# Eight early gate/up half blocks for nine, and the query side's exponential-times-key-sum product on GpSimd

## The chip, the cores and the metric

The kernel runs on one core of a Trainium2 chip. The metric is the time of one execution on the device, in microseconds (us), as the median of several runs. Engines are named as in the profile: PE is TensorE (matmuls; PEld its weight loads), DVE is VectorE, ACT is ScalarE, POOL is GpSimd, SP is SyncE, which issues most DMAs. Each engine works through its own queue in order; semaphores make it wait for the others.

## What is computed

With x of 2048 rows by 576 columns, 32 heads of 18 and a hidden width of 4608, all in f32:

```python
xn = layernorm(x)
q, k, v = split(xn @ wqkv)                       # 32 heads of 18
pq, pk = q @ w_phi, k @ w_phi                    # per head
phi_q = [softmax(pq), softmax(-pq)]; phi_k = [softmax(pk), softmax(-pk)]
kv = phi_k^T v;  z = sum over rows of phi_k      # per head
o = (phi_q kv) / (phi_q z + 1e-6)
s = o @ wo
g = silu((silu(xn @ w_gate) * (xn @ w_up)) @ w_down)
out = x + s * g
```

## The kernel before

**Stages.** A first stage normalizes x and prepares weights (0 to 60 us of the span). A key/value stage makes phi_k, kv and z (to 216 us). A *query stage* makes phi_q, o and s (its transposes run to 447 us). Then comes the gated network: hidden width in NF = 36 blocks of 128 columns, first for rows 0 to 1023 (half i = 0, to about 1010 us), then for rows 1024 to 2047 (i = 1), and a short finish. Matmul operands are split into a high part and a low part, so that a product is made of several matmuls: `split` (lines 72 to 74) casts on ACT and subtracts on DVE.

**Blocks of gate and up.** `gate_up` makes one block of one half by a recursive scheme of 7 products instead of 8, each of 7 matmuls of 512 columns (`product`, line 1014). Some half blocks are made early instead, in the plain way, by `early_tile` (lines 141 to 153; matmuls in line 108): for two row groups j, a gate and an up product of 14 matmuls each, a SiLU (line 147), a product on DVE (line 151) and a store to `h_dram`. They give TensorE work while the attention stages wait on other engines. `EARLY` is the number of blocks that are early in half 1, `FIRST = (EARLY + 1, EARLY)` the number in half 0 and half 1: five and four, nine half blocks. In the network's stage, an early half block is loaded by `stored` instead of being made.

**Weights of the other blocks.** `gate_up_weights` makes a block's parts from raw weights the first time and keeps them in `w_dram` for half 1; a block that was early in half 0 but isn't in half 1 is made there from raw weights. The last rows of the weights are handled apart: `tails(n)` prepares a group of four blocks, with four subtractions on POOL (lines 810 to 813), a cast on ACT (815), a difference on DVE (816) and twelve DMAs issued by POOL (819) into `t_dram`. There are `TAILS` = 8 groups, each tied to a query tile.

**The query stage** works on 16 tiles of 128 rows, in pairs. `q_tile` makes 28 matmuls of 288 columns into `p` (line 108); then on DVE the maximum and minimum per head (530) and two differences (531); two exponentials on ACT (534) into `e`; on DVE the sums of `e` per head (538), the product `ez` of `e` and the key sums `zb` (832), its sums per head (834), five small steps (836 to 841) and the scaling of `e` (842). `numer` transposes `e` of both tiles of a pair on TensorE (854) for each of five groups of heads, splits the result (`ph` on ACT, `pl` on DVE), multiplies it by kv (861) and splits again (`oh`, `ol`); `project` multiplies by wo (889). For each pair the program gives the numerator of the pair before, the two query tiles, then the projection.

**What sets the order.** The kernel is written with a tile framework that orders each engine's instructions itself, when the program is built: by priority (position in the program, raised by `high_priority`) among what it takes to be ready, with `issue_after` as an extra condition. So a change in one engine's load changes the order on all of them. Early matmuls fill the places where TensorE would wait.

Of the kernel before, what the change touches and what calls it, by code (L numbers as in the profile page):

```python
# [23 lines left out]
NF = F // P  # L24
# [5 lines left out]
NL = GROUPS[-1][1]  # L30
NK = NL + NL // 2
QS = 256
EARLY = 4
FIRST = (EARLY + 1, EARLY)
TAILS = (NF - EARLY + 3) // 4
LAG = 3
SHORT = range(22, NF - 5, 4)
# [15 lines left out]
def heads(ap):  # L53
    return ap.rearrange("p (h d) -> p h d", d=DH)


def spread(ap, n):
    return ap.unsqueeze(2).to_broadcast([P, n, DH])
# [3 lines left out]
def gated_hedgehog_kernel(ctx: ExitStack, tc, x, w_qk, w_v, consts_in, wo, w_gu, w_tail, w_down, out):  # L62
# [5 lines left out]
    nc = tc.nc  # L68
# [7 lines left out]
    def split_rows(hi, lo, src):  # L76
        nc.scalar.copy(hi, src)
        nc.vector.tensor_sub(lo, src[:, :, 0:2], hi[:, :, 0:2])
        nc.vector.tensor_sub(hi[64:96, :, 2], src[64:96, :, 2], hi[64:96, :, 2])
# [6 lines left out]
    s_dram = dram.tile([S, D], F32, name="s_dram")  # L86
    h_dram = dram.tile([2, FIRST[0], P, HS], F32, name="h_dram")
    x_dram = dram.tile([2, 4, P, 4, P], F32, name="x_dram")
    sum_dram = dram.tile([2, P, 4, 4, 5, P], F32, name="sum_dram")
    w_dram = dram.tile([NF - EARLY, P, 7, 4, P], F32, name="w_dram")  # L90
    t_dram = dram.tile([TAILS, 4, 3, 32, 7, P], F32, name="t_dram")
# [3 lines left out]
    def block(t):  # L95
        return t // HT, (t % HT) // 4, slice((t % 4) * P, (t % 4 + 1) * P)

    def xw(ps, i, j, cols, wh, wl, stationary_x):
        pairs = []
        for k in range(2):  # L100
            b = XB[i][2 * j + k]
            for c in range(2):
                pairs += [(b[:, c, cols], w[:, k, c]) for w in (wh, wl)]
                pairs += [(b[:, 3 + c, cols], wh[:, k, c])]
            pairs += [(b[:, 2, cols], wh[:, k, 2])]
        for n, (a, b) in enumerate(pairs):
            l, r = (a, b) if stationary_x else (b, a)
            last = nc.tensor.matmul(ps, l, r, start=n == 0, stop=n == len(pairs) - 1)  # L108
        return last
# [9 lines left out]
    def early_raw_part(f, m):  # L119
        raw = epool.tile([P, 2, 3, P], F32, name="raw", bufs=2)  # L120
        nc.sync.dma_start(raw, w_gu[f, :, m:m + 2])
        return raw

    def early_place():
        return epool.tile([P, 2, 3, P], F32R, name="wh", bufs=3), epool.tile([P, 2, 2, P], F32R, name="wl", bufs=3)

    def early_weights(f, *behind):
        parts = []
        for m in (0, 2):
            raw = early_raw_part(f, m)  # L130
            parts.append(early_place())
            with ExitStack() as order:
                for b in behind:
                    order.enter_context(tc.issue_after(b.ins))
                with tc.high_priority():
                    split_rows(*parts[-1], raw)
        return parts
# [3 lines left out]
    def early_tile(f, i, parts, js=(0, 1), banks=None, store=nc.sync, behind=None):  # L141
        for j in js:
            pg, pu = banks or [eps.tile([P, BT], F32, name="pe") for _ in range(2)]
            xw(pg, i, j, slice(0, BT), *parts[0], False)
            h = epool.tile([P, BT], F32, name="h")
            with tc.high_priority():
                silus.append(nc.scalar.activation(h, pg, AF.Silu))
            last = xw(pu, i, j, slice(0, BT), *parts[1], False)
            with tc.issue_after(behind.ins) if behind else ExitStack():
                with tc.high_priority():  # L150
                    nc.vector.tensor_mul(h, pu, h)
            store.dma_start(h_dram[i, f, :, j * BT:(j + 1) * BT], h)
        return last

    outs = []
    with ExitStack() as att:
# [18 lines left out]
        with ExitStack() as wst:  # L175
# [4 lines left out]
            with ExitStack() as pst:  # L180
# [15 lines left out]
                xns, ws, wv, halves = {}, {}, {}, {}  # L196
# [328 lines left out]
            def softmax_parts(ps, e):  # L525
                m = kk_pool.tile([P, 2, H], F32, name="m", bufs=1)
                p4 = ps[:, :, 0:HALF].rearrange("p a (h d) -> p a h d", d=DH)
                for s, op in enumerate((ALU.max, ALU.min)):
                    m3 = m[:, s].rearrange("p (a h) -> p a h", a=2)
                    nc.vector.tensor_reduce(m3, p4, axis=AX.X, op=op)  # L530
                    read.append(nc.vector.tensor_sub(e[:, s * D:(s + 1) * D].rearrange("p (a h d) -> p a h d", a=2, d=DH),
                                                     p4, m3.unsqueeze(3).to_broadcast([P, 2, H // 2, DH])))
                for s in range(2):
                    last = nc.scalar.activation(e[:, s * D:(s + 1) * D], e[:, s * D:(s + 1) * D], AF.Exp,
                                                scale=1.0 if s == 0 else -1.0)
                exps.append(last)
                sm = kk_pool.tile([P, 2 * H], F32, name="sm")
                nc.vector.reduce_sum(sm, heads(e), axis=AX.X)
                return sm
# [142 lines left out]
            order = [6, 7, 0, 1, 2, 3, 4, 5]  # L682
# [63 lines left out]
        with ExitStack():  # L746
# [3 lines left out]
            zb = qc.tile([P, 2 * D], F32, name="zb")  # L750
# [33 lines left out]
        with ExitStack() as qst:  # L784
# [38 lines left out]
            def q_tile(t):  # L823
                i0, j0, cols = block(t)
                pq = qps.tile([P, 2, 512], F32, name="p2")
                for i in range(2):
                    w = slice(i * HALF, (i + 1) * HALF)
                    xw(pq[:, i, 0:HALF], i0, j0, cols, QH[:, :, :, w], QL[:, :, :, w], True)
                e = qk.tile([P, 2 * D], F32, name="e", bufs=4)
                r = softmax_parts(pq, e).rearrange("p (s h) -> p s h", s=2)  # L830
                ez = qk.tile([P, 2 * D], F32, name="ez", bufs=1)
                nc.vector.tensor_mul(ez, e, zb)
                y = qk.tile([P, 2 * H], F32, name="y")
                nc.vector.reduce_sum(y, heads(ez), axis=AX.X)
                y2 = y.rearrange("p (s h) -> p s h", s=2)
                nc.vector.scalar_tensor_tensor(y2[:, 0], r[:, 0], DEN_EPS, y2[:, 0], op0=ALU.mult, op1=ALU.add)
                nc.vector.tensor_mul(y2, y2, r[:, ::-1])
                den = qk.tile([P, H], F32, name="den")
                nc.vector.tensor_add(den, y2[:, 0], y2[:, 1])
                nc.vector.reciprocal(den, den)  # L840
                nc.vector.tensor_mul(y2, r[:, ::-1], den.unsqueeze(1).to_broadcast([P, 2, H]))
                last_e.append(nc.vector.tensor_mul(heads(e), heads(e), spread(y, 2 * H)))
                return e
# [54 lines left out]
            order = list(range(S // QS // 2, S // QS)) + list(range(S // QS // 2))  # L898
# [13 lines left out]
                with tc.issue_after(last_e[3 * n // 2 + 2].ins):  # L912
                    tails(n, exps[NT + 3 * n // 2 + 2])

        for f, halves in [(1, (0,)), (0, (0,))] + [(f, (1, 0)) for f in range(2, EARLY)]:
            parts = first_weights.pop() if f == 1 else early_weights(
                f, *{0: read[2 * NT + 1:2 * NT + 2], 2: (read[2 * NT + 3], exps[NT + 1])}.get(f, ()))
            for i in halves:
                early_tile(f, i, parts, (1,) if f == 1 else (0, 1), behind=read[2 * NT + 1] if f == 1 else None)
# [38 lines left out]
    def gate_up_weights(i, f, ld=None):  # L958

        parts, wt = {}, wts[0]  # L960
        wts.reverse()
        n, q = divmod(f - EARLY, 4)
        raw = i == 0 or f < FIRST[0]
        if raw:
# [3 lines left out]
        def ready(m, src):  # L968
            k = 1 if m == 6 else 2
            w = fw.tile([P, k, 4, P], F32R, name=f"w{k}", bufs=2 if k == 1 else 4)  # L970
            if not raw:
                nc.sync.dma_start(w.bitcast(F32), w_dram[f - EARLY, :, m:m + k])
            else:
# [16 lines left out]
        else:  # L990
            ready(2, ld[:, 2:4] if raw else None)
        held = {0: silus[-2:-1], 2: tops[0:1], 3: tops[1:2]}.get(f - FIRST[0]) if i == 0 else None

# [6 lines left out]
        elif i == 0 and f in SHORT:  # L1000
            later.append(lambda: last(copies[-1:]))
        elif (i, f) == (0, FIRST[0] + 3):
            opened.append(lambda: ready(6, ld[:, 1:2]))
# [416 lines left out]
    for i in range(2):  # L1420
        order = [NF - 1] * i + list(range(FIRST[0], NF - i))
        if i:
            order.insert(NF // 2, EARLY)
        for f in range(FIRST[i]):
            order.insert(4 * f + 1 - i, f)
        units += [(i, n, f) for n, f in enumerate(order)]
# [34 lines left out]

    todo = [(i, f) for i, n, f in units if f >= FIRST[i] and (i == 0 or f < NF - 1)]
    kept = []
    parts = early_weights(EARLY)
    first_rows = [acc[:, 1].rearrange("p (a b) n -> p a (b n)", a=2)[:, n] for n in range(2)]
    for t, f in zip(first_rows, (FIRST[0], 0)):
        nc.sync.dma_start(t, w_down[f * P:(f + 1) * P, :])
    xo = operands(0)
    early_tile(EARLY, 0, parts, store=nc.gpsimd)
    early_raw = [raw_weights(f) for _, f in todo[0:2]]  # L1470
    with tc.issue_after(outs[-3].ins):
        ready = [gate_up_weights(*todo.pop(0), early_raw.pop(0))]
# [84 lines left out]
```

## Time and profile before

| | |
|---|---|
| median of 3 runs | 1579.47 us (1579.38 to 1579.89) |
| the profiled execution | 1580.98 us, its span 1579.2 us |
| granted TensorE clock | 1.00 |
| PE, DVE, ACT, POOL busy | 99%, 74%, 46%, 43% of the span |
| matmuls recorded | 9371 |

A profile's page groups instructions by line, engine, operation and tiles; "x16 | 21.6, 1350 | 0.0" reads: sixteen of them, 21.6 us in all, 1350 ns on average, no idle time of the engine ahead of them. A matmul is recorded with its whole way through the array, while the next one follows sooner: the pace is read from a chain, "1.59 PE px L1014 x7".

### The profile page before, as it was taken

How to read it: one execution, taken by the hardware profiler on the slowest of the kernel's cores; microseconds unless marked ns; L12 is line 12 of the kernel's file. 1: busy time of each engine (PE TensorE's matmuls, PEld its weight loads, DVE VectorE, ACT ScalarE, POOL GpSimd, SP SyncE). 2: the span in 40 equal slices, each digit the busy share in tenths (PEclk: the TensorE clock that was granted, in tenths of full speed). 3: DMA queues.
4: the chain of work that ended last, by engine and by line, in shares of the span. 5: the costliest groups of instructions: out<-in, count | busy, mean ns of one | idle time of the engine just before them, and what ended most of it. 6: DMA issues, size and time to landing. Idle time of an engine off the chain costs nothing.

```text
span 1579.2 us, 25305 instructions
## 1 busy us (share of the span) xinstructions
PE 1570.4 (99%) x9371; PEld 1415.5 (90%) x9371; DVE 1162.8 (74%) x1722; ACT 729.0 (46%) x1408; POOL 671.5 (43%) x723
## 2 busy tenths in 40 slices
PE   9999999999999999999999999999999999999998
PEld 7999999999988898898888888888888888888887
DVE  7777769999947787987777778545766667666577
ACT  6633344545445644444544444454333343333334
POOL 5766653334125545563644444313323324133133
PEclk9999999999999999999999999999999999999999
DMA  9424343336357455454545543964545655555445
GB/s 284 142 67 165 135 154 117 105 118 209 120 185 259 159 181 198 161 182 174 186 161 202 177 168 125 355 210 139 155 146 157 193 173 161 175 184 187 145 118 182
DMA packets 123287, 269.05 MB, mean 170 GB/s; under 512 B 12436, under 2 KB 54100, under 8 KB 121884
## 3 DMA queue, kind: packets, MB, share of 16 engines
q1 hardware_dynamic: 110572, 246.57, 47.6%
q0 software_dynamic: 3552, 12.59, 2.8%
q10 hardware_dynamic: 9040, 8.28, 1.6%
q8 instruction: 74, 1.21, 0.3%
q14 instruction: 49, 0.40, 0.1%
HBM read 167.54 MB, written 99.09 MB: 169 GB/s over the span
## 4 chain that ended last, share of the span: by engine, by line
PE 96%; POOL 1%; DVE 1%; DMA 1%; issue 1%; ACT 0%; SPq 0%; DVEq 0%; POOLq 0%; ACTq 0%
PE px L1014 25%; PE pd L1136 25%; PE pw L1014 12%; PE p L108 6%; PE py L1014 6%; PE pe L108 5%; PE p L889 4%; PE kvp L547 2%; PE pt L861 2%; PE pe L50 1%; PE vx L636 1%; PE pt L854 1%; PE tp L50 1%; PE vw L636 1%; DMA wst<-in_A_w_qk 0%
## 5 line engine op out<-in xcount | busy, mean ns | idle before, releaser
L1136 PEld LDWEIGHTS pd<-dw,hh 128*128 128x128 f32 x3000 | 421.8, 188 | 19.8 <-DVE acc L1372 0.8
L1136 PE MATMUL pd<-dw,hh 128*128 128x288 f32 x3000 | 435.7, 294 | 0.0
L1014 PE MATMUL px<-X,w 128*128 128x512 f32 x1512 | 385.6, 390 | 0.0
L1014 PEld LDWEIGHTS px<-X,w 128*128 128x128 f32 x1512 | 274.6, 188 | 46.1
L1014 PE MATMUL pw<-X,w 128*128 128x512 f32 x744 | 188.8, 389 | 0.0
L1014 PEld LDWEIGHTS pw<-X,w 128*128 128x128 f32 x744 | 139.5, 188 | 28.9
L1372 DVE TENSOR_TENSOR acc<-pd,acc 128x576 f32<-128x576 f32 x128 | 96.4, 753 | 93.3 <-PE pd L1136 92.6
L1047 DVE TENSOR_TENSOR s<-pw,s 128x512 f32<-128x512 f32 x126 | 86.4, 687 | 89.5 <-ACT s L1042 78.9
L1042 ACT COPY s<-px 128x512 f32<-128x512 f32 x126 | 73.6, 584 | 144.9 <-PE px L1014 144.7
L73 ACT CAST hh<-ha 128x512 fp32r<-128x512 f32 x139 | 82.2, 620 | 94.2 <-PE pd L1136 68.7
L74 DVE TENSOR_TENSOR hh<-ha,hh 128x512 fp32r<-128x512 f32 x139 | 111.8, 829 | 18.8 <-ACT hh L73 18.5
L1344 POOL TENSOR_TENSOR hb<-hb 128x512 f32<-128x512 f32 x34 | 46.6, 1372 | 157.2 <-DVE hb L1059 156.8
L74 DVE TENSOR_TENSOR w<-ld,w 128x512 fp32r<-128x512 f32 (+1 forms) x96 | 76.9, 803 | 38.6 <-ACT w L73 37.7
L1014 PE MATMUL px<-X,wt 128*128 128x512 f32 x252 | 98.0, 389 | 0.0
L1014 PE MATMUL py<-X,w 128*128 128x512 f32 x378 | 96.5, 390 | 0.0
L1357 POOL TENSOR_TENSOR ha<-ha 128x512 f32<-128x512 f32 x34 | 52.3, 1554 | 100.1 <-DVE hh L74 94.7
L1331 POOL TENSOR_TENSOR h<-ha,hb 128x512 f32<-128x512 f32 x34 | 44.5, 1309 | 107.2 <-DVE ha L1063 76.4
L983 POOL TENSOR_TENSOR ts<-ld 128x256 f32<-128x256 f32 x32 | 26.8, 839 | 139.6 <-issue 67.4
L73 ACT CAST w<-ld 128x512 fp32r<-128x512 f32 (+1 forms) x96 | 52.7, 550 | 70.3 <-POOL ld L986 40.6
L1067 ACT COPY py<-px 128x512 f32<-128x512 f32 x63 | 36.0, 572 | 106.1 <-PE px L1014 94.6
L108 PE MATMUL pe<-X,wh 128*128 128x512 f32 x260 | 80.4, 395 | 0.0
L1014 PEld LDWEIGHTS py<-X,w 128*128 128x128 f32 x378 | 68.3, 188 | 10.8
(325 smaller groups left out, 3242.3 us busy)
## 6 DMA issues: line engine op xcount, KB each, us to landing
w_dram<-w SPq DMA_DIRECT2D x90, 512.0 KB, 2.6
w<-w_dram SPq DMA_DIRECT2D x90, 512.0 KB, 4.3
wt<-t_dram SPq DMA_DIRECT2D x62, 336.0 KB, 4.4
ld<-in_B_w_gu SPq DMA_DIRECT2D x32, 512.0 KB, 6.3
rt<-in_B_w_down SPq DMA_DIRECT2D x33, 288.0 KB, 5.1
rb<-in_B_w_down SPq DMA_DIRECT2D x33, 288.0 KB, 3.3
w_dram<-w SPq DMA_DIRECT2D x30, 256.0 KB, 2.1
w<-w_dram SPq DMA_DIRECT2D x30, 256.0 KB, 2.7
```

Source lines behind the costliest of these rows:

```text
L73: cast = nc.scalar.copy(hi, src)
L74: return cast, nc.vector.tensor_sub(lo, src, hi)
L108: last = nc.tensor.matmul(ps, l, r, start=n == 0, stop=n == len(pairs) - 1)
L889: nc.tensor.matmul(ps[:, 0:HALF], a, bw, start=k == 0, stop=k == len(mm) - 1)
L1014: nc.tensor.matmul(ps, l, r, start=first and n == 0, stop=last and n == len(mm) - 1, skip_group_check=True)
L1042: snaps.append(nc.scalar.copy(t, ps))
L1047: nc.vector.tensor_add(t, ps, t)
L1136: nc.tensor.matmul(ps, l, r, start=first and n == 0 and m == 0, stop=n == len(hs) - 1 and m == 2, skip_group_check=True)
L1331: sub(s, g["h"][0][0], g["h"][0][1])
L1344: nc.gpsimd.tensor_add(a21, a21, g["h"][1][1])
L1357: sub(a12, a12, g["h"][0][0])
L1372: adds.append(nc.vector.tensor_add(a2, pd[:, :, 0:HALF], a2))
```

## The change

`EARLY` becomes 3 and `FIRST` (5, 3): the early half blocks are now blocks 0 to 4 in half 0 and 0 to 2 in half 1, eight in all. Block 3 of half 1 is made by `gate_up` from raw weights, as block 4 was already; `w_dram` and `t_dram` begin with block 3, so that `TAILS` becomes 9. The product `ez` is issued to POOL.

```diff
-EARLY = 4
-FIRST = (EARLY + 1, EARLY)
+EARLY = 3
+FIRST = (EARLY + 2, EARLY)
 TAILS = (NF - EARLY + 3) // 4
...
                 ez = qk.tile([P, 2 * D], F32, name="ez", bufs=1)
-                nc.vector.tensor_mul(ez, e, zb)
+                nc.gpsimd.tensor_mul(ez, e, zb)
                 y = qk.tile([P, 2 * H], F32, name="y")
                 nc.vector.reduce_sum(y, heads(ez), axis=AX.X)
...
-        for f, halves in [(1, (0,)), (0, (0,))] + [(f, (1, 0)) for f in range(2, EARLY)]:
+        for f, halves in [(1, (0,)), (0, (0,))] + [(f, (1, 0)) for f in range(2, EARLY)] + [(EARLY, (0,))]:
...
         if i:
-            order.insert(NF // 2, EARLY)
+            for f in range(EARLY, FIRST[0]):
+                order.insert(NF // 2 + 4 * (f - EARLY), f)
...
-    parts = early_weights(EARLY)
+    parts = early_weights(FIRST[0] - 1)
...
-    early_tile(EARLY, 0, parts, store=nc.gpsimd)
+    early_tile(FIRST[0] - 1, 0, parts, store=nc.gpsimd)
```

Three places show how the order changes. On DVE, at tile 4 (the second of pair 2), where the row L842 scales `e` of tile 3 and `tl` belongs to a tail, before:

```order
L842 TENSOR_TENSOR e<-e,y 128x1152
L531 TENSOR_TENSOR e<-p_2704,m 128x576
L816 TENSOR_TENSOR tl<-tl,th 128x896
L538 TENSOR_REDUCE sm<-e 128x64
L832 TENSOR_TENSOR ez<-e,zb 128x1152
L834 TENSOR_REDUCE y<-ez 128x64
L836 SCALAR_TENSOR_TENSOR y<-sm,y 128x32
```

and after:

```order
L531 TENSOR_TENSOR e<-p_2704,m 128x576
L841 TENSOR_TENSOR y<-sm,den 128x64
L842 TENSOR_TENSOR e<-e,y 128x1152
L74 TENSOR_TENSOR ol<-pt,oh 126x256
L538 TENSOR_REDUCE sm<-e 128x64
L834 TENSOR_REDUCE y<-ez 128x64
L816 TENSOR_TENSOR tl<-tl,th 128x896
L836 SCALAR_TENSOR_TENSOR y<-sm,y 128x32
```

L832 is gone from DVE, and L834, which now waits for POOL, stands directly behind L538; L816 has moved behind both.

On TensorE, at the end of tile 6's products (`p_2967`), before:

```order
L108 MATMUL p_2967<-QL,X_67 128x288
L108 MATMUL p_2967<-QH,X_67 128x288 x2
L108 MATMUL pe<-X_67,wl 128x512
L861 MATMUL pt<-ph,KVH 126x256 x2
L861 MATMUL pt<-ph,KVL 126x256 x2
L861 MATMUL pt<-pl,KVH 126x256 x2
L889 MATMUL p<-WOH,oh 128x288
```

and after:

```order
L108 MATMUL p_2967<-QH,X_67 128x288 x2
L108 MATMUL p_2967<-QL,X_67 128x288
L108 MATMUL p_2967<-QH,X_67 128x288 x2
L889 MATMUL p<-WOH,ol 128x288
L889 MATMUL p<-WOH,km 128x288
```

Eleven of the 56 projections L889 now stand ahead of these products, with the last L861 of the numerator; 45 follow them.

On POOL, in the query stage, as a piece of the difference (before with -, after with +):

```order
+L832 TENSOR_TENSOR ez<-e,zb 128x1152 x2
+L819 DMA t_dram<-th 32x896 x7
+L832 TENSOR_TENSOR ez<-e,zb 128x1152
+L819 DMA t_dram<-th 32x896
 L819 DMA t_dram<-tl 32x896 x4
 L819 DMA t_dram<-th 32x896 x8
+L832 TENSOR_TENSOR ez<-e,zb 128x1152
 L819 DMA t_dram<-tl 32x896 x4
+L832 TENSOR_TENSOR ez<-e,zb 128x1152
```

The sixteen `ez` now stand among the issues of the tails' DMAs.

## The prediction

> **What bounds the kernel now.** I read the page's busy table first, then a table of windows, then the chain of waits around one pair of query tiles.
>
> ```profile
> span 1579.2 us, 25305 instructions
> PE 1570.4 (99%) x9371; PEld 1415.5 (90%) x9371; DVE 1162.8 (74%) x1722; ACT 729.0 (46%) x1408; POOL 671.5 (43%) x723
> core 0: us, PE busy (x) PEld busy (x) DVE busy (x) ACT busy (x) POOL busy (x), PEclk, DMA share, GB/s
> 219.00:437.00 218.00, 217.62 (x1464) 202.38 (x1464) 202.33 (x314) 107.37 (x175) 71.13 (x134) 1.00 0.46 142
> 437.00:478.00 41.00, 41.00 (x225) 35.08 (x224) 19.36 (x29) 18.09 (x35) 13.19 (x17) 1.00 0.62 207
> 478.00:1555.00 1077.00, 1077.00 (x5968) 956.49 (x5967) 763.49 (x1096) 486.00 (x957) 428.90 (x388) 1.00 0.54 177
> ```
>
> TensorE has work all the time at a granted clock of 1.00: a matmul saved is time saved, and a TensorE wait added is time lost. The one stretch with a second engine near its limit is 219 to 437 us, the query stage, where DVE is busy 202.33 of 218 us (93%). The change touches just this stage. The profiled execution took 1580.98 us, 1.8 more than its span; the median of the three runs shown, 1579.47, lies 1.5 below it. I add the sum to 1580.98 and take 1.5 off.
>
> Pair 3 (tiles 5 and 6) shows how closely the two engines run together. First TensorE's chain, then DVE's rows (start, length).
>
> ```profile
> 287.59 1.60 PE p L108 x12
> 290.13 7.44 PE p L889 x56
> 297.57 0.22 PE pt L854 x2
> 297.79 3.72 PE p L108 x28
> 301.51 1.16 PE pe L108 x5
> 302.67 0.39 PE pt L854 x2
> ```
>
> ```profile
> 290.17 0.75 DVE L530 TENSOR_REDUCE m<-p 128x32 f32<-128x576 f32 x1
> 290.83 0.42 DVE L74 TENSOR_TENSOR ol<-pt,oh 126x256 fp32r<-126x256 f32 x1
> ...
> 292.85 0.76 DVE L531 TENSOR_TENSOR e<-p,m 128x576 f32<-128x576 f32 x1
> ...
> 294.16 1.36 DVE L842 TENSOR_TENSOR e<-e,y 128x1152 f32<-128x1152 f32 x1
> 295.44 1.34 DVE L538 TENSOR_REDUCE sm<-e 128x64 f32<-128x1152 f32 x1
> 296.70 1.35 DVE L832 TENSOR_TENSOR ez<-e,zb 128x1152 f32<-128x1152 f32 x1
> 298.08 1.35 DVE L834 TENSOR_REDUCE y<-ez 128x64 f32<-128x1152 f32 x1
> ...
> 301.08 1.52 DVE L842 TENSOR_TENSOR e<-e,y 128x1152 f32<-128x1152 f32 x1
> ```
>
> Tile 6's products end at 289.19; the transposes that need its finished `e` begin at 302.67; the last DVE step on `e` ends at 302.60. TensorE arrives 0.07 us after the data. Its own work in between (56 products L889, two transposes, 28 products of tile 7, five early ones) fills 13.5 us. Over the stage it loses almost nothing to this:
>
> ```profile
> PEld pt L861 <- DVE pl L74: 1.1, 5, 0.3
> PEld pt L854 <- DVE e L842: 0.6, 2, 0.4
> ```
>
> So there is no reserve: DVE's chain and TensorE's program end together.
>
> **The change part by part.**
>
> *One early half block less, one more in the recursive form.* An early half block is 2 x 2 x 14 = 56 matmuls of 512 columns; the same block in `gate_up` takes 7 x 7 = 49. Seven go.
>
> ```profile
> 456.98 10.89 PE pe L108 x48
> 500.07 1.59 PE px L1014 x7
> ```
>
> ```profile
> L74 DVE TENSOR_TENSOR w<-ld,w 128x512 fp32r<-128x512 f32 (+1 forms) x96 | 76.9, 803 | 38.6 <-ACT w L73 37.7
> ```
>
> The first two rows give 0.227 us each, so 7 x 0.227 = **-1.6 us**. The other costs of block 3 in the second half (a load of raw weights, a tail load, four casts and four differences on DVE, four on POOL, three copies from PSUM; a stored block's load and store go) fall in 478 to 1555 us, where TensorE was busy 1077.00 of 1077.00 us while DVE had 29% free and ACT and POOL more than half, and block 4 was already made there from raw weights. I take 0. Without that cover it would be the differences, 4 x 0.8 = 3.2 us. The stage after the queries begins 12.7 us earlier (56 x 0.227); the order of the program leaves 41 early products there behind the last projection (47 before), and 437 to 478 us has no TensorE wait, so I take 0, with up to 2 us if the opening weights come late.
>
> *The ninth tail.* Four subtractions and twelve DMA issues on POOL, one cast on ACT, one difference on DVE (1.08).
>
> ```profile
> L819 POOL DMA_DIRECT2D t_dram<-th x64 | 31.5, 499 | 53.6 <-ACT th L815 30.2 <-ACT so L895 22.4 <-issue 0.2
> L811 POOL TENSOR_TENSOR tl<-tl 128x128 f32<-128x128 f32 x8 | 5.0, 626 | 0.6
> L816 DVE TENSOR_TENSOR tl<-tl,th 128x896 f32<-128x896 f32 x8 | 8.7, 1083 | 0.0
> ```
>
> 12 x 0.5 + 4 x 0.6 = 8.4 us of POOL, beside 71 busy of 218: 0 by itself. It ends the queue of `ez`, in the last pair.
>
> *`ez` on POOL.* DVE loses 16 x 1.350 = 21.6 us. POOL's price for just this shape (two f32 tensors of SBUF, 128x1152) stands in another stage:
>
> ```profile
> L1407 POOL TENSOR_TENSOR X<-X,acc x2: 2668/2672/2675, 991.6 to 1549.5; 128x1152 f32<-128x1152 f32 x2
> L832 DVE TENSOR_TENSOR ez<-e,zb 128x1152 f32<-128x1152 f32 x16 | 21.6, 1350 | 0.0
> L538 DVE TENSOR_REDUCE sm<-e 128x64 f32<-128x1152 f32 x16 | 21.6, 1347 | 1.6 <-ACT e L534 1.4
> L534 ACT ACTIVATE e<-e 128x576 f32<-128x576 f32 x32 | 21.9, 687 | 17.1 <-DVE e L531 16.2 <-DVE y L841 0.8
> L151 DVE TENSOR_TENSOR h<-pe,h 128x512 f32<-128x512 f32 x10 | 6.8, 685 | 3.8 <-PE pe L108 3.8
> ```
>
> POOL's 2.67 starts with the last exponential, as DVE's 1.35 of L538 does. DVE then waits at L834 for 2.67 - 1.35 = 1.32 us, unless the order puts work between, and behind L834 wait the splits `pl`, `ol`, the next tile's L530 and the chain to `e`. In DVE's changed order L834 follows L538 directly in ten of the sixteen tiles (1, 3, 4, 5, 6, 8, 10, 12, 14, 16); in the other six, 0.7 to 1.4 us of splits stand there. In tiles 4, 10 and 14 the low-ranked L816 stands right *behind* L834: the order does not reckon with a wait there.
>
> What the waits cost is decided by TensorE's new order. For pair 3 it puts 11 of the 56 L889 ahead of tile 6's products; 45 x 0.133 + 0.22 + 3.72 + 1.16 = 11.1 us are left between them and the transposes (13.5 before). DVE's chain there, by the rows above: 0.2 to begin, 3.1 to the end of L531 (3.44 less the `ol`, now elsewhere), 1.9 to the end of tile 5's L842, 1.26 for L538 (start to start), 4.1 from L834 to the end of L842 (298.08 to 302.60, less 0.4 by which POOL stretched two of them): 10.5. A margin of 0.6, if `ez` were ready in time. It is ready at 0.7 (the exponential) + 2.67 and two hand-overs of some 0.1 = 3.6 after L531, where L538 ends at 1.9 + 1.26 = 3.2: 0.5 late, if POOL can start at once. But it seems that it can't while DVE runs L842, which also reads two SBUF tensors:
>
> ```profile
> 236.13 0.45 POOL L812 TENSOR_TENSOR tl<-tl 128x128 f32<-128x128 f32 x1
> 237.68 1.45 POOL L811 TENSOR_TENSOR tl<-tl 128x128 f32<-128x128 f32 x1
> 237.31 1.50 DVE L842 TENSOR_TENSOR e<-e,y 128x1152 f32<-128x1152 f32 x1
> ```
>
> The POOL operation of 0.46 us ends 0.3 after L842 does: it sat through it. With L842 first, `ez` runs from 1.9 to 4.7 and L834 is 1.6 late.
>
> The Trainium skill, page "SBUF — State Buffer", section "SBUF: two separate sides", speaks against the change in the same way: GpSimd and a DVE operation with two SBUF inputs hold the shared port pair for a whole instruction, and the second one blocks. The three rows agree with it.
>
> The sum of the waits, pairs 2 to 8 (pair 1 has 20 us between products and transposes):
> - tiles 3 and 5, whose late L834 holds the pair's second tile or its splits: 2 x 1.3 = 2.6
> - tiles 8 and 16, with no L842 between: 2 x 1.3 = 2.6
> - tiles 4, 6, 10, 12, 14, behind an L842: 5 x 1.6 = 8.0 with the exclusion (5 x 0.5 = 2.5 without)
> - less a margin like pair 3's in seven pairs: 7 x 0.6 = -4.2
>
> 9.0 with the exclusion, 3.5 without; I take **9.0**, as the rows show one operation sitting through the other. Ends: 0 (all covered; at most 0.4 better, the 0.38 us that TensorE idles in the stage), and 16 x 1.32 = 21.
>
> Sum: -1.6 + 9.0 = +7.4 us: 1588.4 for a profiled execution, **1587 us** for the median. TensorE's stage gets shorter by 12.7 us, but only by some 4 of it in time.
>
> **The rivals.**
>
> *All of it hidden* (not slower). DVE's ledger speaks for it: 202.3 - 21.6 - 1.4 (two products L151 less) + 1.1 = 180.4 of a stage of 205.3 us leaves 24.9 us, more than the 10 x 1.32 of direct waits. Then only the seven matmuls count: 1579.5 - 1.6 = 1577.9. Against it: the work left between products and transposes was cut by as much, 13.5 to 11.1 in pair 3. Chance 0.26.
>
> *`ez` behind the tails' DMAs.* In POOL's queue every `ez` from tile 7 on stands behind three or more issues L819. A group begins when ACT's cast of its tail is done (53.6 us of idle ahead of the 64 issues). Where that cast is done only with the exponential, some five issues of 0.5 go first, 2.5 us a tile; in half of the ten tiles that is 12.5 on top of the forecast, 1599.5. It decides only there; in ACT's order most of these casts stand several places ahead of the exponential. Chance 0.07.
>
> *A gain beyond the seven matmuls.* TensorE idles 0.38 us in the stage and its two waits on DVE make 1.7; even with all of it gone, 1576.2 is the floor. Chance 0.04 for 1576.3 or less.
>
> *The change doesn't do what it says*: TensorE's changed order has 308 early products for 364 and 49 more in `gate_up`, and the sixteen `ez` stand in POOL's queue. I give it nothing.
>
> **How the numbers follow.** Forecast (waits of 3.5 to 14 us): 0.63, 1581.4 to 1592; hidden 0.26; behind the DMAs 0.07; gain 0.04. The range from 1577.3 to 1592 takes in the hidden case and the waits up to 14, and leaves out the DMA case, the far end of 21 and the floor. About 0.2% (3.2 us: 1576.3 to 1582.6) is what a measurement of this kernel tells from no change. Slower: 0.07 and nearly all of the forecast, less its low end near 3.5 (0.05), 0.65; the same: hidden and that end, 0.31; faster 0.04.
>
> **What would show it.** Right: 7 matmuls fewer; `ez` 2.7 us on POOL, 4 beside an L842; idle time of DVE ahead of L834 put down to POOL `ez`, some 15 us; TensorE's idle time in the query stage up from 0.4 to some 9 us, at `pt` behind `e` L842 and `pl`. Wrong: TensorE's idle time stays under 2 us (then the slack was there, 1577.9); or POOL's `ez` starts long after the exponential, behind L819; or TensorE waits at the opening after the last projection, which I took as 0.

## The result and the profile after the change

The changed kernel takes **1621.4 us** (median of four runs, 1620.6 to 1622.53), the kernel before in the same comparison 1579.7 (1579.4 to 1583.2): a ratio of 1.0259, 95% interval 1.0242 to 1.0277. It is 41.7 us slower, where 7.4 were forecast and 1592 was the upper end of the range. The page of the profile after:

```profile
span 1619.0 us, 25350 instructions
PE 1579.3 (98%) x9364; PEld 1419.8 (88%) x9364; DVE 1151.9 (71%) x1713; ACT 727.9 (45%) x1412; POOL 726.4 (45%) x759
```

Seven matmuls went (9371 to 9364), as the change says. POOL is busy 54.9 us more, 45.0 of them the `ez`. DVE is busy only 10.9 us less, though the `ez` were 21.6 there: other work came in, that of block 3 and of the ninth tail in part. Next the windows of TensorE in three stages: the query stage, the opening of the gated network, the rest.

```profile
core 0: us, PE busy (x), PEclk, DMA share, GB/s
216.00:440.00 224.00, 200.24 (x1314) 0.97 0.44 134
440.00:510.00 70.00, 68.09 (x384) 1.00 0.59 194
510.00:1560.00 1050.00, 1043.50 (x5775) 1.00 0.54 175
```

Idle time is the length less PE's busy time: 23.8 us, 1.9 us and 6.5 us, where the kernel before has 0.4, 0 and 0. (A matmul's row reaches past the start of the next, so that idle time is a little under what is lost.) In the first stage the mean granted clock fell as well, to 0.97. Which waits these are, from the answer on waits between 216 and 480 us (total, number, longest):

```profile
DVE y L834 <- POOL ez L832: 21.1, 14, 7.0
...
PE pt L854 <- DVE e L842: 14.6, 8, 6.1
...
PE p L108 <- DVE e L531: 7.0, 1, 7.0
...
PE pt L861 <- DVE pl L74: 2.5, 3, 1.4
```

and after 480 us:

```profile
PE px L1014 <- ACT s L1042: 6.3, 3, 2.4
```

Two single waits, of 7.0 and 6.1 us, stand out of others of at most 2.4; a third place, small but repeated, lies in the last rows. **The first**, at 233 us, by the timeline; POOL's rows, then ACT's and DVE's, then TensorE's, each from its own answer:

```profile
233.31 0.46 POOL L810 TENSOR_TENSOR tl<-tl 128x128 f32<-128x128 f32 x1 [9.38 <-DMA h_dram<-h]
233.72 2.61 POOL L832 TENSOR_TENSOR ez<-e,zb 128x1152 f32<-128x1152 f32 x1
```

```profile
224.77 1.26 ACT L534 ACTIVATE e<-e 128x576 f32<-128x576 f32 x2
...
236.37 1.35 DVE L834 TENSOR_REDUCE y<-ez 128x64 f32<-128x1152 f32 x1 [6.96 <-POOL ez L832]
...
237.64 0.75 DVE L530 TENSOR_REDUCE m<-p 128x32 f32<-128x576 f32 x1
```

```profile
241.02 0.58 PE L108 MATMUL p<-QH,X 128*128 128x288 f32 x1 [7.00 <-DVE e L531]
```

The exponentials of tile 1 end at 226.0, but its `ez` starts at 233.72. The tail's first subtraction L810 stands ahead of it in POOL's queue, and its load has not landed:

```profile
L808 SPq DMA_DIRECT2D tl<-in_B_w_tail x2: 408/440/473, 226.7 to 227.1; - x2
...
DMA to landing us min/median/max: 6.5/6.5/6.5
```

226.7 + 6.5 = 233.2, which is when L810 could start. (Its row names another transfer, the store of `h`; the releaser is inferred, and the load's landing fits the time.) L810 waited for this load before the change too, with only the tail's own work behind it. Now DVE waits 6.96 us at L834, L530 of tile 2 stands behind that, the PSUM buffer that L530 and L531 read stays occupied, and TensorE waits for L531.

**The second**, at 339 us, by the timeline of all engines (SPq and ACTq are the DMA issues of SP and ACT):

```profile
326.28 2.92 SPq L947 DMA_DIRECT2D X<-sum_dram  x5
...
329.82 2.85 SPq L947 DMA_DIRECT2D X<-sum_dram  x3
...
330.21 0.33 ACTq L896 DMA_DIRECT2D s_dram<-so  x1
...
332.94 0.75 DVE L531 TENSOR_TENSOR e<-p,m 128x576 f32<-128x576 f32 x1
...
338.18 0.40 ACT L895 COPY so<-p 128x288 f32<-128x288 f32 x1 [5.81 <-DMA s_dram<-so]
338.47 0.69 ACT L534 ACTIVATE e<-e 128x576 f32<-128x576 f32 x1
```

The copies `so` have two buffers, and this one needs back the buffer of the last copy but one, whose store was issued at 330.21, amid eight loads X<-sum_dram. It can start only 8 us after that issue. The second exponential of tile 8 stands behind the copy in ACT's queue, though its input (L531) was ready at 333.7; `e` of tile 8 is late by that, and TensorE waits for it. Sixteen such loads fill the operands of the network's stage as soon as the early blocks of half 1 release the buffers. Half 1's early blocks now end with block 2, so that in SP's order the first eight stand behind the first pair's `km` transfers (line 869) and the second eight, these, behind the third's; before, they stood behind the fourth's to the sixth's.

**The third**, twice in the second half (near 1332 and 1402 us) and 1.4 us long in the first: `px` is the PSUM tile of a `gate_up` product and `s` its copy on ACT. Each from its own answer:

```profile
1326.05 1.03 POOL L983 TENSOR_TENSOR ts<-ld 128x256 f32<-128x256 f32 x1 [4.40 <-DVE sx L1372]
```

```profile
1331.13 0.60 ACT L73 CAST w<-ld 128x512 fp32r<-128x512 f32 x1
1331.63 0.58 ACT L1042 COPY s<-px 128x512 f32<-128x512 f32 x1
...
1332.26 1.67 PE L1014 MATMUL px<-X,w 128*128 128x512 f32 x6 [2.41 <-ACT s L1042]
```

ACT's casts `w` of a block's raw weights follow POOL's operations L983 to L986, of which the first starts 4.4 us after POOL came free; the copy `s`, which TensorE needs, stands behind the casts.

### The profile page after: what moved, and what is told of

Same layout as the page of the kernel before. It is cut to its first block, busy times and chain, and to the rows that moved or that the text cites. A ratio compares the mean times of both kernels' runs of the same rounds, so it can differ in the third digit from the quotient of the medians.

```text
span 1619.0 us, 25350 instructions
## 1 busy us (share of the span) xinstructions
PE 1579.3 (98%) x9364; PEld 1419.8 (88%) x9364; DVE 1151.9 (71%) x1713; ACT 727.9 (45%) x1412; POOL 726.4 (45%) x759
## 4 chain that ended last, share of the span: by engine, by line
PE 65%; POOL 1%; DMA 0%; DVE 0%; issue 0%; ACT 0%; SPq 0%; DVEq 0%; POOLq 0%; ACTq 0%
PE pd L1136 24%; PE px L1014 24%; PE pw L1014 12%; PE py L1014 6%; DMA rt<-in_B_w_down 0%; PE px L1136 0%; POOL ld L986 0%; ACT w L73 0%; POOL ts L984 0%; POOL ts L983 0%; DMA out<-ts 0%; POOL ld L985 0%; ACT py L1054 0%; PE pw L1136 0%; PE py L1136 0%
## 5 line engine op out<-in xcount | busy, mean ns | idle before, releaser
L1014 PE MATMUL px<-X,w 128*128 128x512 f32 x1536 | 392.3, 390 | 6.3 <-ACT s L1042 6.3
L1014 PEld LDWEIGHTS px<-X,w 128*128 128x128 f32 x1536 | 279.2, 188 | 53.9 <-ACT s L1042 7.0
L832 POOL TENSOR_TENSOR ez<-e,zb 128x1152 f32<-128x1152 f32 x16 | 45.0, 2812 | 94.7 <-ACT e L534 94.7
L983 POOL TENSOR_TENSOR ts<-ld 128x256 f32<-128x256 f32 x33 | 27.9, 844 | 112.7 <-issue 70.3
```

The costliest lines, as they stand in the source:

```text
L832: nc.gpsimd.tensor_mul(ez, e, zb)
L1014: nc.tensor.matmul(ps, l, r, start=first and n == 0, stop=last and n == len(mm) - 1, skip_group_check=True)
```

## The experiments

The ratios of the experiments stand against runs of the kernel before on the same chip (1580.1 to 1580.3 us). Idle time of TensorE is from the same three windows as above, worked out in the same way. It is that of the one profiled execution, which lies within 1.3 us of the median but for e7 (2.1 over it), e9 (3.1 over) and e8 mended (3.5 under). An early product is one matmul of an early half block, 0.227 us.

| run | us | ratio to before (95%) | idle 216 to 440 | 440 to 510 | 510 to 1560 |
|---|---|---|---|---|---|
| kernel before | 1579.7 | | 0.4 | 0.0 | 0.0 |
| changed kernel | 1621.4 | 1.0259 (1.0242 to 1.0277) | 23.8 | 1.9 | 6.5 |
| e1 half blocks alone | 1603.2 | 1.0149 (1.0132 to 1.0166) | 0.5 | 10.8 | 4.8 |
| e2 `ez` alone | 1607.2 | 1.0170 (1.0155 to 1.0186) | 19.8 | 1.4 | 0.4 |
| e3 `ez` first | 1617.3 | 1.0234 (1.0219 to 1.0249) | 19.9 | 1.9 | 6.7 |
| e5 X late | 1614.2 | 1.0216 (1.0201 to 1.0232) | 19.4 | 2.3 | 6.3 |
| e6 half 1 later | 1614.8 | 1.0217 (1.0202 to 1.0233) | 23.3 | 1.9 | 2.6 |
| e7 these three | 1603.1 | 1.0142 (1.0125 to 1.0159) | 16.1 | 2.2 | 1.9 |
| e9 e7, `ez` in two pieces | 1597.3 | 1.0111 (1.0096 to 1.0126) | 9.8 | 3.8 | 0.0 |
| e10 e7, a piece on each engine | 1592.5 | 1.0077 (1.0062 to 1.0092) | 5.3 | 5.5 | 0.0 |
| e8 half blocks alone, mended | 1595.5 | 1.0091 (1.0076 to 1.0106) | 0.9 | 9.1 | 0.0 |
| e8 held | 1595.3 | 1.0089 (1.0072 to 1.0106) | 9.2 | 2.4 | 0.7 |
| e12 nine half blocks, a piece each | 1587.0 | 1.0044 (1.0029 to 1.0059) | 5.4 | 0.0 | 0.0 |

### Each part alone

The changed kernel with `ez` on DVE:

```diff
-                nc.gpsimd.tensor_mul(ez, e, zb)
+                nc.vector.tensor_mul(ez, e, zb)
```

> The changed kernel with `ez` back on DVE: eight early half blocks alone. Theory (several separate costs): the profile after shows TensorE waiting 7.8 us more in 478 to 1600 us (6.1 of it for the raw weights of blocks 3 and 4 in half 1), which belongs to the half blocks, so 1579.7 - 1.6 + 7.8 = about 1586 us, with up to 9 us more if the loads X<-sum_dram, which the change brings 90 us forward, hold up a store here too. Rival (all of the loss is the late `ez`): only the seven matmuls count, about 1578 us.

Measured 1603.2, 23 us over the kernel before: both theories missed it. The query stage is nearly free of waits, the third stage loses its 4.8, and the opening, which neither theory had named, loses most. TensorE's windows there:

```profile
216.00:440.00 224.00, 223.52 (x1498) 1.00 0.48 146
440.00:510.00 70.00, 59.23 (x290) 0.95 0.63 216
```

10.8 us idle, and 5% of 70 us (3.5) to the clock. The program's order suggests why: behind the last projection it leaves no early product, where the kernel before leaves 48 and the changed one 42. The last pair and the first weights are then uncovered; e8 held, below, tries this.

The kernel before with `ez` on GpSimd:

```diff
-                nc.vector.tensor_mul(ez, e, zb)
+                nc.gpsimd.tensor_mul(ez, e, zb)
```

> The kernel before with `ez` on GpSimd: nine early half blocks, the product moved. Theory: 7.2 us for the first `ez`, which stands in POOL's queue behind a tail's first subtraction (L810) that waits for its load, and about 13 us of waits at `pt` and `pl` in the later pairs: 1579.7 + 20 = about 1600 us; X<-sum_dram is loaded late as before, so no wait of ACT for a store of s. Rival 1 (the waits need the thinner cover of eight half blocks): 1587 us or less. Rival 2 (`ez` makes the whole loss): about 1621 us.

Measured 1607.2, 27 us over: the theory fell 7 short, and both rivals are out. With nine half blocks to cover it, the query stage still idles 19.8 us, with the 7 us wait of the first `ez` and no burst of loads. 103 early products are left behind the last projection: in both orders with `ez` on POOL only 180 stand between the first transposes and the last tile's products, where the kernel before has 211. So the cover is there and isn't used. That the order takes DVE to be relieved and does not reckon with waits at L834 would explain it; this was not tried.

The parts do not add: 23 + 27 = 50, and together they cost 41.7. `ez` on POOL leaves the early products for the opening that the half blocks alone lack; the early loads of X hurt only beside it.

### Three single edits

```diff
-                sub(t[:, 4], t[:, 2], t[:, 0])
+                with tc.issue_after(ezs[1].ins): sub(t[:, 4], t[:, 2], t[:, 0])
...
-                nc.gpsimd.tensor_mul(ez, e, zb)
+                ezs.append(nc.gpsimd.tensor_mul(ez, e, zb))
```

> The changed kernel with the first two `ez` ahead of the tails' first subtractions in POOL's queue; the other four engines' queues are the same, row for row. Theory: the wait of 7.16 us of TensorE at 233 us goes, about 1614 us, and the first `ez` ends 3 us or so after its exponential. Rival (the tail's chain is late instead, and something behind it waits, since POOL's subtractions now wait for the second `ez`): within 2 us of 1621.

4.1 us came back, not 7.2: the wait of 7.0 shrank to 1.9, and the granted clock after it is still 0.66 over 237 to 242 us. What is left shows on DVE, which had this split (L78) beside the `ez`; its group, with shortest, median and longest time, in this run between 222 and 236 us, and `ez` from the timeline:

```profile
L78 DVE TENSOR_TENSOR wl<-raw,wh x2: 681/1918/3155, 226.3 to 226.9; 128x512 fp32r<-128x512 f32 x2
```

```profile
226.42 3.07 POOL L832 TENSOR_TENSOR ez<-e,zb 128x1152 f32<-128x1152 f32 x1 [2.18 <-ACT e L534]
```

The second of the two splits started at 226.9, with `ez` under way, and took 3.16 us in place of 0.68: it ended 0.6 us after `ez` (229.49). This is the exclusion of the prediction from the other side: DVE sat through POOL's instruction. The Trainium skill, page "SBUF — State Buffer", section "SBUF: two separate sides", says just this, that the one that starts second blocks until the other is done; the two rows agree.

```diff
-                nc.sync.dma_start(rows[:, a], src[:, a])
+                with ExitStack() if i else tc.issue_after(kms[{6: 7, 3: 9, 5: 11, 4: 13}[n]].ins): nc.sync.dma_start(rows[:, a], src[:, a])
```

(`kms` collects the DMAs of line 869, two for each pair.)

> The changed kernel with the sixteen loads X<-sum_dram held back in SP's queue behind the fourth to seventh pair's loads of km, about as before the change; the other four engines' queues are the same, row for row. Theory: ACT's copy `so` no longer waits 5.8 us for the store of s behind a burst of these loads, so the wait of 6.26 us of TensorE at 339 us goes, and with it the 2.8 us lost to the granted clock of 0.75 at 345 to 351 us: about 1612 us. Rival (the store is slow for another reason, or the loads hit another store): over 1619 us.

1614.2, 7.2 us less (9 expected). The long wait at `pt` is gone; the answer on waits of 216 to 480 us has for it now

```profile
PE pt L854 <- DVE e L842: 10.0, 8, 1.7
```

in place of 14.6 with a longest of 6.1. So the burst of loads made the store slow.

```diff
-                order.insert(NF // 2 + 4 * (f - EARLY), f)
+                order.insert(NF // 2 + 1 + 4 * (f - EARLY), f)
```

> The changed kernel with blocks 3 and 4 of half 1 one place later each, so that their raw weights are made in units that have no late finish of an earlier block; TensorE's and POOL's queues keep their rows. Theory (ACT's casts of the weights stand behind POOL's subtractions, those behind the late finish, and ahead of ACT's copy `s` that the next product waits for): both waits of 2.57 us at `px` in half 1 go, and the 0.8 us or so behind each: about 1615 us. Rival (the casts, differences and subtractions cost this wherever they stand): within 1.5 us of 1621.

1614.8, 6.6 us less. Of the three waits at `px` after 480 us one is left, in half 0:

```profile
PE px L1014 <- ACT s L1042: 2.2, 1, 2.2
```

So the raw weights of blocks 3 and 4 cost this at their place, not by themselves. In e6 the copy `s` comes first (1329.74) and the next cast of `ld` only at 1337.45. POOL's L983 comes no sooner, 5.1 us after POOL came free, so that the late finish of an earlier block (line 1112), to which the expectation put its lateness, is not shown to be the reason; nothing here tried it apart.

### The three together

> The changed kernel with three edits together: the first two `ez` ahead of the tails' subtractions, the loads X<-sum_dram late, blocks 3 and 4 one place later. Theory (separate costs): 1621.4 less the 4.1 and 7.2 measured for the first two alone, less 6 for the third: about 1604 us, and what is left against before is the 13 to 15 us of waits at `pt` and `pl`. Rival (one hides another): over 1608 us.

1603.1: the costs add (4.1 + 7.2 + 6.6 = 17.9, measured 18.3), as expected. What is left in the query stage:

```profile
PE pt L854 <- DVE e L842: 11.7, 9, 1.7
PE pt L861 <- DVE pl L74: 2.5, 3, 1.4
PE p L108 <- DVE e L531: 1.9, 1, 1.9
...
DVE y L834 <- POOL ez L832: 14.2, 13, 1.5
```

(The last row is from the answer on all engines.) DVE waits 14.2 us at L834, 1.3 to 1.5 us in each of nine tiles and less in four. TensorE waits 11.7 + 2.5 us at `pt`. Of these, 1.7 us belong to pair 1, which has no wait at L834 left (DVE's split L78 there took 2.07 us beside the `ez` of tile 2); in pairs 2 to 8 it is 12.5 us, so that most of what DVE loses there reaches TensorE.

### Is it POOL's lateness?

`ez` of e7 in two pieces of one tile, both on POOL (e9), or the second on DVE (e10):

```diff
-                ezs.append(nc.gpsimd.tensor_mul(ez, e, zb))
+                nc.gpsimd.tensor_mul(ez[:, 0:D], e[:, 0:D], zb[:, 0:D]); ezs.append(nc.gpsimd.tensor_mul(ez[:, D:2 * D], e[:, D:2 * D], zb[:, D:2 * D]))
```

> As the run with the three edits, with `ez` made in two pieces of 128x576, the first as soon as the first of the two exponentials is done. POOL's 2.67 us then begin 0.69 us earlier and should end some 2.0 us behind the last exponential, so that DVE's L834 waits about half as long. Theory (the waits at `pt` and `pl` come from POOL's lateness at L834): they fall from 13 to 15 us to some 7, 6 to 8 us faster than the run with the three edits. Rival (they come from the thinner cover, 180 early products in place of 211 ahead of the last tile's products): within 1.5 us of it.

> As the run with the three edits, with the first piece of `ez` on POOL and the second on DVE: POOL's piece (about 1.35 us) is done 0.7 us behind the last exponential, before DVE's L538 ends. DVE gets 16 x 0.68 = 10.9 us back; the order then leaves 26 early products behind the last projection for 42. Theory (lateness at L834 makes the waits, and early products behind the last projection cover the opening): the waits at `pt` and `pl` all but go, the opening loses at most (42 - 26) x 0.227 = 3.6 us: 10 to 14 us faster than the run with the three edits, 1590 to 1594 us. Rival (TensorE's waits come with the thinner cover, or POOL and DVE hold each other up in the two pieces): within 4 us of it.

e9: 1597.3, 5.8 us less than e7, just short of the 6 to 8 expected. The same rows:

```profile
PE pt L854 <- DVE e L842: 6.5, 6, 2.3
...
DVE y L834 <- POOL ez L832: 2.9, 5, 1.0
```

TensorE's order is nearly the same as in e7, with the same 180 and 42 early products, but DVE's waits at L834 fell from 14.2 to 2.9 us and TensorE's at `pt` nearly halved. So the lateness makes most of them. e10: 1592.5, 10.6 less than e7 and within what was expected; the answer on waits has none at L834 any more, and `pt` has 3.1 us. It pays at the opening, which keeps 26 early products of 42:

```profile
440.00:510.00 70.00, 64.48 (x319) 0.98 0.67 228
```

5.5 us idle for 2.2 in e7. With the 98 early products that nine half blocks leave there, this goes too:

> The kernel before (nine half blocks) with the first piece of `ez` on POOL and the second on DVE, and the first two pieces ahead of the tails' subtractions. The order leaves 98 early products behind the last projection, so the opening is covered. Theory: what the run of the eight half blocks with `ez` split between the engines lost in the query stage, some 5 to 6 us more than before, is all that is left: about 1586 us. Rival (with nothing late at L834 the nine half blocks cover everything): 1580 us or less.

```profile
216.00:440.00 224.00, 218.65 (x1486) 1.00 0.44 133
440.00:510.00 70.00, 70.00 (x353) 1.00 0.73 242
```

1587.0, as expected. The missing half block is thus worth 5.5 us here (1592.5 less 1587.0). What remains is 5.35 us of idle time in the query stage, where 184 early products stand between the first transposes and the last tile's products and the kernel before has 211; what makes it was not tried. No version here beats the kernel before.

### Is it the cover?

The half blocks alone (e1) with X late and half 1 later, and then with the last early half block held behind the last projection:

```diff
-    early_tile(FIRST[0] - 1, 0, parts, store=nc.gpsimd)
+    with tc.issue_after(pes[-1].ins): early_tile(FIRST[0] - 1, 0, parts, store=nc.gpsimd)
```

(`pes` collects the matmuls of line 889.)

> The eight half blocks alone (`ez` on DVE) with the loads X<-sum_dram late and blocks 3 and 4 of half 1 one place later. TensorE's order leaves no early product behind the last projection (48 before the change, 42 in the changed kernel). Theory (the opening, 440 to 500 us, loses about 17 us for want of these products): only the 5 to 6.6 us of half 1 go, 1603.2 - 6 = about 1597 us. Rival (the early burst of X loads or the raw weights make the opening late): under 1590 us.

> As the run of the mended half blocks alone, with the 56 products of the last early half block held behind the last projection; the query stage then has 56 early products fewer. Theory (early products are a store that is spent once): the opening's 17 us go, and up to 56 x 0.227 = 12.7 us of waits appear in the query stage: 1592 to 1598 us, with no wait over 2 us in 455 to 500 us. Rival 1 (the opening waits for weights whatever TensorE has): 1609 us or so. Rival 2 (the query stage has slack): about 1580 us.

1595.5 and 1595.3: the same time, and the idle time changed its place. Mended, then held:

```profile
216.00:440.00 224.00, 223.13 (x1494) 1.00 0.48 146
440.00:510.00 70.00, 60.87 (x305) 0.98 0.66 226
```

```profile
216.00:440.00 224.00, 214.81 (x1444) 0.98 0.48 145
440.00:510.00 70.00, 67.63 (x342) 0.98 0.66 224
```

The opening's 9.1 us fell to 2.4, and the query stage's 0.9 rose to 9.2. So early products are a store that is spent once, and with eight half blocks and `ez` on DVE it does not reach. The loss is 1595.5 - (1580.3 - 1.6) = 16.8 us, where the dropped half block took away 56 x 0.227 = 12.7 us of cover. The profiled execution was faster, 1592.0, and lost 13.3: 10.0 of idle time, 1.4 to the clock (0.98 over the opening's 70 us), and 1.9 that these windows do not show.

## Why the prediction was wrong

The direction was right, and one chain was the one that was forecast: DVE waits at L834, and TensorE at `pt`. The sum was +7.4, measured +41.7. By its steps:

- **The matmuls, -1.6**: right in number (9364). But the ninth half block was worth more as cover than its seven matmuls: its going costs 16.8 us with `ez` on DVE (e8 mended), and 5.5 with `ez` on both engines (e10 against e12).
- **"pair 1 has 20 us between products and transposes"**, by which the first pair was left out of the sum: this failed by 7.0 us of waiting and its clock. The room behind tile 1's products is no help where tile 2's products need the same PSUM buffer read. The rival on POOL's queue looked at the DMA issues L819 only, and asked only from tile 7 on; what stood ahead of the first `ez` was L810, which waits for a load. A row of the kernel before showed it:

```profile
235.17 0.47 POOL L810 TENSOR_TENSOR tl<-tl 128x128 f32<-128x128 f32 x1 [9.64 <-DMA h_dram<-h]
```

- **SP's queue** got no term. The step said that a stored block's load and store go, but not that half 1's early blocks end one block sooner, which releases the X buffers to sixteen loads. Price: 7.2 us (e5), and only with `ez` on POOL in the same kernel: e1 has the early loads too, without a long wait in the query stage.
- **Second half, taken as 0** on 29% idle DVE and idle ACT and POOL: 6.6 us. An engine's mean idle time did not cover a queue in which a waiting cast stands ahead of a copy that TensorE needs. One place later neither wait is left in the second half (e6), so the 0 was right for the work and wrong for its place.
- **The waits, 13.2 gross less a margin of 4.2**: the gross figure was right, and in the tiles that were named. Those nine waited 12.1 us at L834 in e7, each 1.3 to 1.5; four more (9, 11, 13, 15), left out because splits stand there, add 2.1. The margin did not exist: 0.6 a pair was worked out for pair 3 alone, and that pair's transposes wait 1.5 us in e7. TensorE lost 12.5 us in pairs 2 to 8, where 9.0 were forecast.
- **The exclusion, 5.5 us of the sum**, was seen, and cost less. Not five but four `ez` ran beside an L842 (tiles 6, 10, 12 and 14); they took 0.9, 0.2, 0.5 and 0.9 us longer than the 2.66 of the others, 2.5 us in all. Tile 6 of the changed kernel:

```profile
306.35 1.36 DVE L842 TENSOR_TENSOR e<-e,y 128x1152 f32<-128x1152 f32 x1
306.68 3.56 POOL L832 TENSOR_TENSOR ez<-e,zb 128x1152 f32<-128x1152 f32 x1 [3.36 <-ACT e L534]
...
310.26 1.35 DVE L834 TENSOR_REDUCE y<-ez 128x64 f32<-128x1152 f32 x1 [1.29 <-POOL ez L832]
```

- **The opening, 0**: within the 2 us that it allowed (1.9), and for the reason given, the early products left there. The step did not see that they are there only because the query stage goes without them.
- **The rival "all of it hidden"**, at 0.26, counted DVE's ledger, 24.9 us of room. In the changed kernel 21.1 us of DVE's idle time are waits at L834 for POOL.

All `ez` on POOL in the changed kernel (shortest, median, longest in ns):

```profile
L832 POOL TENSOR_TENSOR ez<-e,zb x16: 2611/2666/3557, 233.7 to 453.6; 128x1152 f32<-128x1152 f32 x16
```

So the failed step is the list of what waits behind what: the sum priced one kind of wait in seven pairs, and put at nothing the first `ez` in POOL's queue, the loads of X that are released sooner, and the place of the raw weights in the second half. These three make 18.3 us. The other 23.4 are, in e7, 14.2 us of idle time at `pt` (12.5 by the forecast's own mechanism, with no margin), 1.9 us at `p` behind the split that sat through `ez`, and 4 us of idle time after 440 us, less the 1.6; how much of the last belongs to `ez` was not tried apart, and some 5 us are put down to nothing here.

## What to carry to other kernels

An instruction that moves to another engine takes over that queue's waits: look up what stands ahead of it there, for the first use as well, and which of those wait for a load. Work that fills an engine's waits is a store spent once; cut it, or let the order keep it back, and the idle time turns up where it was last needed, so that two parts of a change are not to be priced apart. Where an automatic order is built on one engine's load, ask whether it knows how long the moved work takes elsewhere; two pieces that start earlier gained 5.8 us here at no change in the engine.

## What the runs showed of the hardware

A wait of TensorE can cost more than its length. After the 7.0 us wait of the changed kernel the granted clock was 0.50 for five microseconds of work:

```profile
235.00:240.00 5.00, 0.00 (x0) 0.92 0.06 22
240.00:245.00 5.00, 3.98 (x17) 0.50 0.00 0
245.00:250.00 5.00, 5.00 (x27) 0.90 0.26 74
```

(1 - 0.50) x 4 + (1 - 0.90) x 5 = 2.5 us on top. The Trainium skill, page "TensorE: Matmul & The Clock Gate", part 1, has half rate after an idle window of about 3.4 us and full rate after a busy one; these rows agree. But in e1 the clock fell where no wait between 437 and 447 us was longer than 1.1 us:

```profile
440.00:445.00 5.00, 2.81 (x21) 1.00 0.14 52
445.00:450.00 5.00, 4.58 (x26) 0.66 0.33 74
```

Here three waits, of 1.1, 1.1 and 0.4 us, within some 5 us were enough. One wait of 2.4 us can be, and need not be: the changed kernel has it twice in the second half, ending at 1332.3 and at 1401.6, and the clock fell after the second alone:

```profile
1335.00:1340.00 5.00, 5.00 (x30) 1.00 0.39 95
...
1403.00:1407.00 4.00, 4.00 (x18) 0.57 0.39 142
```

So waits shorter than that window cost clock too, where they fall badly or come close together. The kernel before, with at most 0.4 us of idle time in each of the three windows, was granted 1.00 in all of them.
